# Extra rows of w4 on five DMA engines, wide value matmuls on four column groups, and a reordered tail in a one-token attention kernel

## The chip, the cores and the metric

The kernel runs on one core of a Trainium2 chip. A core has TensorE (PE; its weight loads, which overlap its matmuls, are listed as PEld), VectorE (DVE), ScalarE (ACT), GpSimd (POOL) and SyncE (SP), and 16 DMA engines that move data between memory (HBM) and the on-chip memory. The metric is the device time of one execution in microseconds, the median of several; the profile is of one execution.

## The reference

One token `x` of 512 numbers goes through two branches. Branch A is attention over the last 4096 positions of a cache, with 32 heads of width 128; branch B is a small gated network.

```python
xn = layernorm(x)
# A
q = (xn @ wq)                       # 32 heads x 128
k, v = k_cache[..., -4096:, :], v_cache[..., -4096:, :]
p = softmax(q . k * 128 ** -0.5)
s = concat(p @ v) @ wo              # 4096 -> 512
# B
h = gelu(layernorm(xn) @ w1)        # shifted by one or two tokens: with one token, zeros
x1 = xn + shift(h) @ w2             # so x1 = xn
g = silu(x1 + gelu(layernorm(x1) @ w3) @ w4)   # 512 -> 1376 -> 512
out = x + s * g
```

Everything is bf16 in memory. Keys and values are 32 MB each, wq and wo 4 MB each, w2, w3, w4 and x 3.3 MB: 78.84 MB are read once.

## The kernel before

**Layout.** The heads are taken in 8 groups of G = 4. A group's keys are one tile of 128 partitions by 128 "chunks" of 128 numbers (32 KB in a partition, 4 MB), its values another. `load_kv` (line 97) loads one, whole or in pieces along the chunks (`cuts`); a piece of 64 chunks is 16 KB in each partition. All loads but x's are issued by SP in program order (`load`, line 78), and an issue that must wait for its buffer holds up those behind it. There are three key buffers and two value buffers. The value buffers lie where the first weights (pool `wts`) were, so that the first values wait until queries are made.

**Start.** w2, w3, w4, wq are loaded, then keys. The few operations on x, branch B (lines 177 to 238) and the queries (241 to 258) run meanwhile. w4 is loaded as 10 rows in each of 128 partitions and 96 rows of 1 KB. The planner of the framework orders the operations of this part on each engine; in `manual_schedule` (line 510 on) PE, DVE and ACT run in program order.

**A stage.** Stage `s` (the loop of line 514) takes the keys of group s and the values of group h = s - 2. Of the 128 key chunks DVE takes the first 64 to 80 (`k_vector`, lines 308 and 310: a product and a sum over 128 numbers). For the rest PE turns chunks (line 324), ACT copies them (326) and PE multiplies them with the queries (332). The softmax follows one stage later (`sm_turn`, `sm_exp`, line 370), its denominator (`sm_den`, line 376) two stages later. `v_part` multiplies the probabilities with the values: for most groups as 128 matmuls with the value chunk as stationary operand and four columns moving (line 430), for groups in `MOVED`, here 0 and 2, as 32 matmuls with 16 columns of probabilities stationary and four chunks, 512 columns, moving (line 422); `v_add` (437) then gathers the right four blocks of that result one stage later. `v_out` divides by the denominator.

**Output projection.** The 32 heads are three `blocks`: 16, 8 and 8. For a block `ox_spread` and `ox_pick` (lines 456 to 476) rearrange the heads' outputs so that wo can be loaded with several of its rows in one partition: `y_wide` for block 0 and `y_block` (line 501) for the others, which adds into `y_ps` with four matmuls a row over four column groups (`rows_add`, line 150). Of the last block only 320 rows, `wo_few`, are loaded so: in two loads over an outermost dimension of NE = 5, into 20 partitions each, 8 KB in a partition (line 402), and `ox_few` (line 478) puts the outputs there by a product with the constant `few`. The rest, `wo_rows`, comes as rows of 1 KB, half of head 26 and heads 27 to 31 (`load_rows`); `y_head` multiplies them.

**Tail.** At s = 8 PE runs: softmax of group 7, block 1's `ox_pick` and `y_block(1)`, the sum of block 0's row (line 589), values of group 6, the denominator of group 7, the last block's `ox_pick` and `ox_few`. At s = 9: the first 64 chunks of group 7's values, `y_block` of the few rows, heads 26 and 27, the other chunks, `v_out`, heads 28 to 31. Then the product with `g_row`, the sum with x, the store. SP's order at the end: values 6, rows of heads 26 and 27, values 7 in pieces of 64, 48 and 16 chunks, rows of heads 28 and 29, 30, 31.

Of the kernel before, what the change touches and what calls it, by code (L numbers as in the profile page):

```python
# [8 lines left out]
P = 128  # L9
# [16 lines left out]
MOVED = (0, 2)  # L26
# [3 lines left out]
def kernel(  # L30
# [28 lines left out]
    assert F == 10 * P + 96  # L59
# [30 lines left out]
    w4_sb = wts.tile([P, 11, D], BF16, name="w4_sb")  # L90
    load(w4_sb[:, 0:10, :], B_w4[0:10 * P, :].rearrange("(p c) n -> p c n", p=P))
    load(w4_sb[0:96, 10, :], B_w4[10 * P:F, :])
    wq_sb = wts.tile([P, KC, HD], BF16, name="wq_sb")

    load(wq_sb[:].rearrange("p c n -> p (c n)"), A_wq.rearrange("(a b c) n -> b a (c n)", a=2, c=KC))
# [80 lines left out]

    x_f = small.tile([P, KC], FP32, name="x_f")
# [8 lines left out]
    perm = wts.tile([P, P // 2, 2], BF16, name="perm")  # L186
    nc.vector.tensor_copy(out=perm[:], in_=ident_bf[:].rearrange("k (a b) -> k b a", a=2))
# [24 lines left out]
    chunks = [(P, slice(r, 10 * P, 10)) for r in range(10)]  # L212
    chunks += [(96, slice(10 * P, F, 1))]
    a_ps = ps_misc.tile([P, 11], FP32, tag="misc", name="a_ps")
    for j, (m, cols) in enumerate(chunks):
        for c in range(KC):
            nc.tensor.matmul(a_ps[0:m, j:j + 1], lhsT=w3_sb[:, c, cols], rhs=z3_bf[:, c:c + 1],  # L217
                             start=(c == 0), stop=(c == KC - 1))
    a_bf = small.tile([P, 11], BF16, name="a_bf")
    nc.scalar.activation(out=a_bf[:, 0:10], in_=a_ps[:, 0:10], func=ACT.Gelu_apprx_tanh)  # L220
    nc.scalar.activation(out=a_bf[0:96, 10:11], in_=a_ps[0:96, 10:11], func=ACT.Gelu_apprx_tanh)
# [5 lines left out]
    for i, (m, _) in enumerate(chunks):  # L227
        nc.tensor.matmul(hr_ps[:], lhsT=a_bf[0:m, i:i + 1], rhs=w4_sb[0:m, i, :], start=False,  # L228
                         stop=(i == len(chunks) - 1))
# [31 lines left out]

    few = const.tile([P, 2, 32], BF16, name="few")
    nc.vector.memset(few[:], 0.0)
    for c in range(2):
        nc.vector.tensor_copy(
            out=few[:, c, 0:4 * NE].rearrange("p (a b) -> p a b", b=4),
            in_=ident_bf[:, 4 * NE * c:4 * NE * (c + 1)].rearrange("p (b a) -> p a b", b=4))


# [18 lines left out]
                            op0=ALU.add, op1=ALU.mult)  # L290

# [93 lines left out]
    blocks = [(0, 16), (16, 8), (24, 8)]  # L385
    few_block = 2
    few_h = blocks[few_block][0]
    FEW = 8 * 8 * NE
    h_part = few_h + FEW // P

    r_part = FEW % P
# [6 lines left out]
    def load_few():  # L398
        t = wo_blk[few_block]
        for c in range(2):  # L400
            r0 = few_h * P + c * FEW // 2
            load(t[32 * c:32 * c + 4 * NE],
                 A_wo[r0:r0 + FEW // 2, :].rearrange("(b a t) n -> a b (t n)", b=4, a=NE))

# [3 lines left out]
    def load_rows(h, n):  # L408
        if h == h_part:
            load(wo_rows[r_part:P, 0, :], A_wo[h * P + r_part:(h + 1) * P, :])  # L410
            h, n = h + 1, n - 1
        load(wo_rows[:, h - h_part:h - h_part + n, :],
             A_wo[h * P:(h + n) * P, :].rearrange("(h p) n -> p h n", p=P))
# [3 lines left out]
    def v_part(g, v, c0=0, c1=CP):  # L417
        s = st[g]
        if g in MOVED:
            s["ov"] = ps_o.tile([4 * G, 4, Dh], FP32, tag="oT", name="ov")  # L420
            for c in range(0, CP, 4):
                nc.tensor.matmul(s["ov"][:], lhsT=s["pT"][:, c:c + 4, :].rearrange("p i a -> p (i a)"),  # L422
                                 rhs=v[:, c:c + 4, :], start=(c == 0), stop=(c == CP - 4))
            s["ov_sb"] = sm_pool.tile([4 * G, 4, Dh], FP32, tag="ov_sb", bufs=1, name="ov_sb")
            nc.scalar.copy(out=s["ov_sb"][:], in_=s["ov"][:])  # L425
            return
        if c0 == 0:
            s["oT"] = ps_o.tile([P, G], FP32, tag="oT", name="oT")
        for c in range(c0, c1):
            nc.tensor.matmul(s["oT"][:], lhsT=v[:, c, :], rhs=s["pT"][:, c, :], start=(c == 0),  # L430
                             stop=(c == CP - 1))

    def v_add(g):
        s = st[g]
        s["oT"] = ps_misc.tile([P, G], FP32, tag="misc", name="oT")
        for j in range(4):
            nc.tensor.matmul(s["oT"][:], lhsT=s["ov_sb"][:, j, :], rhs=ident_f[0:4 * G, G * j:G * j + G],  # L437
                             start=(j == 0), stop=(j == 3))

    def v_out(g):  # L440
        h = G * g
        b = [i for i, (h0, _) in enumerate(blocks) if h >= h0][-1]
        if b not in o_blk:
            o_blk[b] = sm_pool.tile([P, blocks[b][1]], BF16, tag=f"o{b}", bufs=1, name="o")
            if b == few_block:
                nc.gpsimd.memset(o_blk[b][:], 0.0)
        c = h - blocks[b][0]
        if g >= NG - 2:
            nc.vector.tensor_tensor(out=o_blk[b][:, c:c + G], in0=st[g]["oT"][:], in1=st[g]["rden"][:],  # L449
                                    op=ALU.mult)  # L450
            return
        for k in range(G):
            nc.scalar.mul(o_blk[b][:, c + k:c + k + 1], st[g]["oT"][:, k:k + 1], st[g]["rden"][:, k:k + 1])  # L453
# [24 lines left out]
    def ox_few(i):  # L478
        of_ps = ps_misc.tile([64, 8], FP32, tag="misc", name="of_ps")
        nc.tensor.matmul(of_ps[:], lhsT=few[:].rearrange("p a b -> p (a b)"), rhs=ox_blk[i][:],  # L480
                         start=True, stop=True)
        of = sm_pool.tile([64, 8], BF16, tag="of", bufs=1, name="of")
        nc.vector.tensor_copy(out=of[:], in_=of_ps[:])
        ox_blk[i] = of


# [14 lines left out]
    def y_block(i):  # L501
        for t in range(8):
            rows_add(y_ps, ox_blk[i][:, t:t + 1], wo_blk[i][:, t, :], False)

    def y_head(h):
        rows_add(y_ps, o_blk[few_block][:, h - few_h:h - few_h + 1], wo_row(h), h == H - 1)

    NG = H // G
    cuts = (0, 64, 112, CP)
# [4 lines left out]
    for s in range(NG + LAG):  # L514
# [3 lines left out]
        if s == LAG:  # L518
            wts_guard.__exit__(None, None, None)
            v_pool = ctx.enter_context(tc.tile_pool(name="v", bufs=V_BUFS))  # L520
            wo_blk[few_block] = v_pool.tile([64, 8, D], BF16, tag="wo_few", bufs=1, name="wo_few")
            nc.gpsimd.memset(wo_blk[few_block][:], 0.0)
            wo_rows = v_pool.tile([P, H - h_part, D], BF16, tag="wo_rows", bufs=1, name="wo_rows")
            nc.gpsimd.memset(wo_rows[0:r_part, 0, :], 0.0)
        if last:
            load_rows(h_part, 2)
# [9 lines left out]
        if h == 5:  # L536
            load_wo(1)
            load_few()
# [41 lines left out]
        elif s == NG:  # L580
# [3 lines left out]
            sm_turn(NG - 1)  # L584
            ox_spread(1)
            sm_exp(NG - 1)
            ox_pick(1)
            y_block(1)
            rows_add(y_ps, one_f, y_row, False)
            v_part(h, v)  # L590
            v_out(h)
            ox_spread(few_block)
            sm_den(NG - 1)
            sm_rden(NG - 1)
            ox_pick(few_block)
            ox_few(few_block)
        else:
            v_part(h, v, 0, cuts[1])
            y_block(few_block)
            for r in range(h_part, H - G):  # L600
                y_head(r)
# [41 lines left out]
```

## Time and profile before

| | us |
|---|---|
| median of 4 runs | 195.05 (194.93 to 196.39) |
| profiled execution | 196.39 |
| its span in the profile | 194.5 |
| PE busy | 133.4 (69%) |
| DVE busy | 143.8 (74%) |
| ACT busy | 87.0 (45%) |
| POOL busy | 6.5 (3%) |
| HBM rate over the span | 405 GB/s |
| values of group 7, first piece issued by SP | 172.73 |
| values of group 6 at PE | 178.80 |
| last matmul of the rows | 191.1 |

The span of the profile is the program on the core; the execution's time holds some 1.9 us more around it. Times on the page and in the timeline are microseconds from the span's start, and "issue" in the chain is time in which an engine waited for nothing that the profile shows. The page gives the busy share in 40 slices of 4.86 us, the chain of work that ended last, and groups of instructions with their mean duration. The timeline lists instructions in order of time with the idle time before them. Where the text speaks of landing marks, they are the marks that each DMA engine sets when its part of a load is in place; a load over all engines has sixteen. Packet durations are of the trace's DMA records, which tell a packet's queue, start, size and duration.

### The profile page before, as it was taken

Reading aid. Unit: us, or ns where it says so; the run is one execution under the profiler, and the core shown is the slowest. Engines: PE = TensorE matmul, PEld = TensorE weight load, DVE = VectorE, ACT = ScalarE, POOL = GpSimd, SP = SyncE. Lnnn points to the kernel's source line nnn. Section 1 sums busy time; section 2 is a strip of 40 time slices with the busy share of each in tenths; the row PEclk is TensorE's granted clock in tenths of the full one; section 3 lists DMA queues with packets and bytes.
Section 4 is the critical chain, followed back from the end, with each engine's and each line's share of the span. In section 5 each row is a group of like instructions: output and inputs, shape, how many; then the busy total and the mean of one; then the engine's idle time right before and its main releaser. Section 6 shows DMA issues by size and latency. Waiting matters only on the chain.

```text
span 194.5 us, 4769 instructions
## 1 busy us (share of the span) xinstructions
PE 133.4 (69%) x2123; PEld 101.9 (52%) x2123; DVE 143.8 (74%) x162; ACT 87.0 (45%) x195; POOL 6.5 (3%) x14
## 2 busy tenths in 40 slices
PE   0559760877856589698898929740788878855782
PEld 0453450766645433487794418730768246744761
DVE  1550119988999999999999999990899989951201
ACT  2003010788896350478678135721475059813000
POOL 2110007000000000000000000000000000000000
PEclk9999855698555558978559985855555599655555
DMA  6999999999999999999999999999999999999980
GB/s 214 415 442 371 377 428 457 431 438 421 438 428 431 438 426 428 431 431 428 425 428 445 421 431 391 472 421 428 425 451 430 425 428 389 470 418 367 425 308 2
DMA packets 4725, 79.13 MB, mean 407 GB/s; under 512 B 666, under 2 KB 1466, under 8 KB 1722
## 3 DMA queue, kind: packets, MB, share of 16 engines
q1 hardware_dynamic: 4554, 78.84, 95.8%
q8 instruction: 16, 0.26, 0.5%
q10 hardware_dynamic: 152, 0.00, 0.0%
q14 instruction: 3, 0.02, 0.0%
HBM read 78.84 MB, written 0.00 MB: 405 GB/s over the span
## 4 chain that ended last, share of the span: by engine, by line
DMA 46%; DVE 34%; PE 11%; ACT 6%; issue 1%; ACTq 0%; SPq 0%
DMA kv<-in_A_k_cache_dram 29%; DVE S L310 20%; DMA kv<-in_A_v_cache_dram 14%; DVE prod L308 11%; PE oT L430 6%; ACT kt L326 5%; PE pt L324 3%; DMA x_bf<-in_A_x_dram 2%; PE y_ps L150 1%; PE sT L332 1%; ACT own L341 1%; DVE S L346 1%; DVE m L348 1%; DVE mx L356 0%; DVE md L358 0%
## 5 line engine op out<-in xcount | busy, mean ns | idle before, releaser
L310 DVE TENSOR_REDUCE S<-prod 128x20 f32<-128x2560 bf16 (+2 forms) x32 | 82.2, 2570 | 1.1
L326 ACT COPY kt<-pt 128x1024 bf16<-128x1024 bf16 (+1 forms) x56 | 54.4, 1007 | 22.6 <-PE pt L324 21.9
L324 PE MATMUL pt<-ident_bf,kv 128*128 128x128 bf16 x444 | 45.1, 268 | 10.3 <-DMA kv<-in_A_k_cache_dram 10.3
L308 DVE TENSOR_TENSOR prod<-kv,q_bc 128x2560 bf16<-128x2560 bf16 (+2 forms) x32 | 43.5, 1359 | 7.9 <-DMA kv<-in_A_k_cache_dram 5.8
L324 PEld LDWEIGHTS <-kv 128*128 128x128 bf16 x444 | 36.5, 123 | 12.4 <-DMA kv<-in_A_k_cache_dram 11.1
L332 PE MATMUL sT<-qT_bf,kt 128*128 128x4 bf16 x444 | 20.6, 168 | 16.6 <-ACT kt L326 15.8
L332 PEld LDWEIGHTS <-kt 128*128 128x128 bf16 x444 | 17.0, 103 | 24.5 <-ACT kt L326 24.4
L430 PE MATMUL oT<-pT,kv 128*128 128x4 bf16 x768 | 22.1, 166 | 6.1 <-issue 4.7
L430 PEld LDWEIGHTS <-kv 128*128 128x128 bf16 x768 | 21.4, 104 | 8.0 <-issue 5.6
L422 PE MATMUL ov<-kv,pT 128*16 128x512 bf16 x64 | 16.5, 423 | 0.0
L370 ACT ACTIVATE pT<-S,mb 128x128 bf16<-128x128 f32 x32 | 13.9, 569 | 0.3
L453 ACT ACTIVATE o<-oT,rden 128x1 bf16<-128x1 f32 x24 | 4.3, 261 | 15.2 <-PE oT L430 8.5
L422 PEld LDWEIGHTS <-pT 128*16 128x16 bf16 x64 | 6.1, 98 | 9.4 <-issue 3.2
L449 DVE TENSOR_TENSOR o<-oT,rden 128x4 bf16<-128x4 f32 x2 | 0.3, 162 | 12.4 <-PE oT L430 12.4
L341 ACT ACTIVATE own<-sT,par 128x48 f32<-128x48 f32 (+2 forms) x32 | 7.6, 361 | 3.7 <-PE sT L332 3.7
L370 ACT ACTIVATION_READ_ACCUMULATOR pT<-S,mb 128x1 f32 x32 | 8.2, 255 | 0.0
L231 DVE COPY hr<-hr_ps 1x512 f32<-1x512 f32 x1 | 0.7, 679 | 8.4 <-PE hr_ps L228 8.4
L496 PE MATMUL yr_ps<-wo,ox 128*1 128x512 bf16 x16 | 6.0, 560 | 0.9 <-DVE ox L474 0.9
L425 ACT COPY ov_sb<-ov 16x512 f32<-16x512 f32 x2 | 1.1, 575 | 12.0 <-PE ov L422 12.0
L437 PE MATMUL oT<-ident_f,ov_sb 16*128 16x4 f32 x16 | 2.9, 301 | 4.3 <-DVE rden L381 4.3
L220 ACT ACTIVATE a_bf<-a_ps 128x10 bf16<-128x10 f32 x1 | 0.2, 180 | 11.8 <-PE a_ps L217 11.8
L363 PE MATMUL mb_ps<-md,par_t 5*128 5x4 f32 x16 | 4.0, 316 | 1.7 <-DVE md L358 1.0
(117 smaller groups left out, 92.6 us busy)
## 6 DMA issues: line engine op xcount, KB each, us to landing
kv<-in_A_k_cache_dram SPq DMA_DIRECT2D x7, 4096.0 KB, 30.5
kv<-in_A_v_cache_dram SPq DMA_DIRECT2D x7, 4096.0 KB, 34.8
wq_sb<-in_A_wq_dram SPq DMA_DIRECT2D x1, 4096.0 KB, 19.7
kv<-in_A_k_cache_dram SPq DMA_DIRECT2D x2, 2048.0 KB, 25.2
wo<-in_A_wo_dram SPq DMA_DIRECT2D x1, 2048.0 KB
kv<-in_A_v_cache_dram SPq DMA_DIRECT2D x1, 2048.0 KB, 11.4
kv<-in_A_v_cache_dram SPq DMA_DIRECT2D x1, 1536.0 KB, 14.4
w_sb<-in_B_w_dram SPq DMA_DIRECT2D x1, 1376.0 KB
```

The lines of the kernel that those rows point to most:

```text
L308: nc.vector.tensor_tensor(out=prod[:, 0:m, :], in0=kn[:, rows, :], in1=q_bc[:, g:g + 1, :].to_broadcast([P, m, Dh]), op=ALU.mult)
L310: nc.vector.tensor_reduce(out=st[g]["S"][:, rows], in_=prod[:, 0:m, :], axis=AX.X, op=ALU.add)
L324: nc.tensor.transpose(pt[:, c - c0, :], kn[:, c, :], ident_bf[:])
L326: nc.scalar.copy(out=kts[b][:, 0:c1 - c0, :], in_=pt[:, 0:c1 - c0, :])
L332: nc.tensor.matmul(st[g]["sT"][:, c - nd(g), :], lhsT=kt[:, c - c0, :], rhs=qT_bf[:, G * g:G * g + G], start=True, stop=True)
L341: nc.scalar.mul(s["own"][:, 0:m, a], s["sT"][:, 0:m, a], par[:, a:a + 1])
L363: nc.tensor.matmul(mb_ps[:], lhsT=par_t[:].rearrange("k b a -> k (b a)"), rhs=md[:], start=True, stop=True)
L370: nc.scalar.activation(out=s["pT"][:, :, a], in_=s["S"][:], func=ACT.Exp, scale=scale, bias=mb[:, a:a + 1], accum_out=s["sum"][:, a:a + 1])
L422: nc.tensor.matmul(s["ov"][:], lhsT=s["pT"][:, c:c + 4, :].rearrange("p i a -> p (i a)"), rhs=v[:, c:c + 4, :], start=(c == 0), stop=(c == ...
L430: nc.tensor.matmul(s["oT"][:], lhsT=v[:, c, :], rhs=s["pT"][:, c, :], start=(c == 0), stop=(c == CP - 1))
L453: nc.scalar.mul(o_blk[b][:, c + k:c + k + 1], st[g]["oT"][:, k:k + 1], st[g]["rden"][:, k:k + 1])
L496: nc.tensor.matmul(yr[i][:], lhsT=ox_blk[i][:, t:t + 1], rhs=wo_blk[i][:, t, :], start=(t == 0), stop=(t == n - 1))
```

## The change

w4 is loaded as 8 rows in each of 128 partitions, 32 rows of 1 KB, and 320 extra rows in the manner of `wo_few`: `w4_few`, cleared by POOL, in two loads over five. w3's columns are taken in the matching order, so the hidden numbers are 17 columns and not 11, and the product with `few` (which moves up) puts the last eight in their places. wq's rows are laid in four parts and not two. wo's last eight heads become a block of 4 (`wo_4`, 128 partitions) and 4 heads of 1 KB rows. Groups 0 to 5 are all `MOVED`; their 32 wide matmuls now write four column groups in turn, 32 partitions apart, after a matmul of zeros that clears the tile, and `v_add` sums the four with the constant `fold`. In the tail, `v_out` of groups 5 on is DVE's, the values of group 6 come ahead of `y_block(1)`, `ox_pick(2)` stands behind the first 64 chunks of group 7, and group 7's values come in pieces of 64, 32, 16 and 16 chunks.

```diff
-MOVED = (0, 2)
+MOVED = (0, 1, 2, 3, 4, 5)
...
-    w4_sb = wts.tile([P, 11, D], BF16, name="w4_sb")
-    load(w4_sb[:, 0:10, :], B_w4[0:10 * P, :].rearrange("(p c) n -> p c n", p=P))
-    load(w4_sb[0:96, 10, :], B_w4[10 * P:F, :])
+    w4_sb = wts.tile([P, 9, D], BF16, name="w4_sb")
+    load(w4_sb[:, 0:8, :], B_w4[0:8 * P, :].rearrange("(p c) n -> p c n", p=P))
+    load(w4_sb[0:32, 8, :], B_w4[F - 32:F, :])
+    w4_few = wts.tile([64, 8, D], BF16, name="w4_few")
+    nc.gpsimd.memset(w4_few[:], 0.0)
+    for c in range(2):
+        f0 = 8 * P + 32 * NE * c
+        load(w4_few[32 * c:32 * c + 4 * NE],
+             B_w4[f0:f0 + 32 * NE, :].rearrange("(b a t) n -> a b (t n)", b=4, a=NE))
...
-    load(wq_sb[:].rearrange("p c n -> p (c n)"), A_wq.rearrange("(a b c) n -> b a (c n)", a=2, c=KC))
+    load(wq_sb[:].rearrange("p c n -> p (c n)"), A_wq.rearrange("(a b c) n -> b a (c n)", a=4, c=KC))
...
+    chunks = [P] * 8 + [32] + [8 * NE] * 8
+    a_ps = ps_misc.tile([P, 17], FP32, tag="misc", name="a_ps")
+    for j, m in enumerate(chunks):
         for c in range(KC):
-            nc.tensor.matmul(a_ps[0:m, j:j + 1], lhsT=w3_sb[:, c, cols], rhs=z3_bf[:, c:c + 1],
+            nc.tensor.matmul(a_ps[0:m, j:j + 1], lhsT=w3_cols(c, j), rhs=z3_bf[:, c:c + 1],
                              start=(c == 0), stop=(c == KC - 1))
...
+    nc.scalar.activation(out=a_bf[0:8 * NE, 9:17], in_=a_ps[0:8 * NE, 9:17], func=ACT.Gelu_apprx_tanh)
+    af_ps = ps_misc.tile([64, 8], FP32, tag="misc", name="af_ps")
+    nc.tensor.matmul(af_ps[:], lhsT=few[0:8 * NE].rearrange("p a b -> p (a b)"), rhs=a_bf[0:8 * NE, 9:17],
+                     start=True, stop=True)
+    af_bf = small.tile([64, 8], BF16, name="af_bf")
+    nc.vector.tensor_copy(out=af_bf[:], in_=af_ps[:])
...
+    fold = const.tile([P, 32], FP32, name="fold")
+    nc.vector.tensor_reduce(out=fold[:], in_=ident_f[:].rearrange("p (q m) -> p m q", m=32), axis=AX.X,
+                            op=ALU.max)
...
-    blocks = [(0, 16), (16, 8), (24, 8)]
+    blocks = [(0, 16), (16, 8), (24, 4), (H - G, G)]
+    h_part = H - G
...
-            s["ov"] = ps_o.tile([4 * G, 4, Dh], FP32, tag="oT", name="ov")
-            for c in range(0, CP, 4):
-                nc.tensor.matmul(s["ov"][:], lhsT=s["pT"][:, c:c + 4, :].rearrange("p i a -> p (i a)"),
-                                 rhs=v[:, c:c + 4, :], start=(c == 0), stop=(c == CP - 4))
+            s["ov"] = ps_o.tile([P, 4, Dh], FP32, tag="oT", name="ov")
+            nc.tensor.matmul(s["ov"][:], lhsT=zero_bf[:], rhs=zero_bf[:].unsqueeze(1).to_broadcast([P, 4, Dh]),
+                             start=True, stop=False, skip_group_check=True)
+            for i in range(CP // 4):
+                c, r = 4 * i, 32 * (i % 4)
+                nc.tensor.matmul(s["ov"][r:r + 4 * G], lhsT=s["pT"][:, c:c + 4, :].rearrange("p i a -> p (i a)"),
+                                 rhs=v[:, c:c + 4, :], start=False, stop=(i >= CP // 4 - 4),
+                                 skip_group_check=True)
...
-            nc.tensor.matmul(s["oT"][:], lhsT=s["ov_sb"][:, j, :], rhs=ident_f[0:4 * G, G * j:G * j + G],
+            nc.tensor.matmul(s["oT"][:], lhsT=s["ov_sb"][:, j, :], rhs=fold[:, G * j:G * j + G],
...
-        if g >= NG - 2:
+        if g >= NG - 3:
...
-    cuts = (0, 64, 112, CP)
+    cuts = (0, 64, 96, 112, CP)
...
-            wo_blk[few_block] = v_pool.tile([64, 8, D], BF16, tag="wo_few", bufs=1, name="wo_few")
-            nc.gpsimd.memset(wo_blk[few_block][:], 0.0)
+            wo_blk[2] = v_pool.tile([P, 4, D], BF16, tag="wo_4", bufs=1, name="wo_4")
...
-            load_rows(h_part, 2)
             v = load_kv(v_pool, A_v_cache, h, cuts)
...
             load_wo(1)
-            load_few()
+            load_wo(2)
...
             sm_turn(NG - 1)
+            sm_exp(NG - 1)
+            v_add(h - 1)
+            v_out(h - 1)
             ox_spread(1)
-            sm_exp(NG - 1)
             ox_pick(1)
+            v_part(h, v)
+            v_out(h)
+            ox_spread(2)
             y_block(1)
             rows_add(y_ps, one_f, y_row, False)
-            v_part(h, v)
-            v_out(h)
-            ox_spread(few_block)
             sm_den(NG - 1)
             sm_rden(NG - 1)
-            ox_pick(few_block)
-            ox_few(few_block)
         else:
             v_part(h, v, 0, cuts[1])
-            y_block(few_block)
-            for r in range(h_part, H - G):
-                y_head(r)
+            ox_pick(2)
+            y_block(2)
             for c0, c1 in zip(cuts[1:], cuts[2:]):
                 v_part(h, v, c0, c1)
             v_out(h)
```

## The prediction

> **What bounds the kernel.** I read the page's slices first, then the queues, then the chain at its end, then the timeline around it.
>
> ```profile
> span 194.5 us, 4769 instructions
> ...
> DMA  6999999999999999999999999999999999999980
> GB/s 214 415 442 371 377 428 457 431 438 421 438 428 431 438 426 428 431 431 428 425 428 445 421 431 391 472 421 428 425 451 430 425 428 389 470 418 367 425 308 2
> ...
> q8 instruction: 16, 0.26, 0.5%
> ```
>
> The loads run from end to end. Every one is issued before its predecessors have landed; the closest is the last values' first piece, issued at 172.73, when the earliest of the 16 engines runs out at 175.2 (its part of the rows before). So a faster compute stage in the middle buys nothing. What can move the end is the work per DMA engine and the chain behind the last values. That chain, in order of time:
>
> ```profile
> 150.71 28.04 DMA kv<-in_A_v_cache_dram
> 178.75 0.05 issue
> 178.80 2.21 PE oT L430 x77
> 181.01 0.13 issue
> 181.14 1.52 PE oT L430 x51
> ...
> 184.34 1.80 PE oT L430 x64
> 186.14 0.41 PE y_ps L150 x9
> 186.55 0.78 issue
> 187.32 1.11 PE y_ps L150 x27
> 188.44 1.81 PE oT L430 x64
> ...
> 190.49 0.62 PE y_ps L150 x15
> ```
>
> TensorE is busy nearly throughout from 178.8 (values of group 6, "V6") to 191.11. The loads' landing marks end in a tie with it: V7's pieces land at 184.12, 187.76 and 188.99, the rows of heads 28-31 at 189.62, 189.94 and 190.26. The result leaves 3.4 us after the last row of the chain.
>
> The "issue" pieces are the other thing to see. q8 brings TensorE's instructions, 16 KB or 256 instructions at a time. I numbered TensorE's instructions in order of time: its unexplained stops before numbers 1729, 2497, 3521, 3777 and 4033 are all multiples of 256 apart, each ending 1.3 to 1.5 us after a q8 packet of 1.05 us. The stop of 187.32 is packet 184.95, the stop of 181.14 packet 178.62. A packet starts 3.4 to 6.2 us after TensorE comes near the block before (1.7 for the very last one, among small loads). A block is 128 matmuls with their weight loads, 3.6 us when dense, so dense stretches outrun the fetch.
>
> ```profile
> 172.43 0.18 PEld L430 LDWEIGHTS <-kv 128*128 128x128 bf16 x4 [1.38 <-issue]
> ...
> 176.06 1.02 PE L150 MATMUL y_ps<-wo,ox 128*1 128x128 bf16 x32 [0.62 <-DVE ox L474]
> ```
>
> **The loads.** Packet durations in the trace: 1 KB 46 ns, 4 KB 159, 8 KB 309, 10 KB 385, 16 KB 613, 32 KB 1213. Each `wo_few` load leaves five landing marks, where others leave sixteen: five engines carry it. Per engine:
> - w4: before 8x385 + 6x46 = 3.36 us on all. After 8x309 + 2x46 = 2.56 on eleven engines and 2.47 more (8x309, the few rows) = 5.03 on five.
> - wo's end: before 12x46 ahead of V7 and 32x46 behind it, plus 2.47 of `wo_few` on five. After 8x159 = 1.27 ahead of V6, 32x46 behind.
>
> The total is 0.08 us less on every engine, and the unevenness moves from 167 us to 10 us. Until V6 the eleven engines are 0.79 early and the five 1.67 late; V6 lands 0.47 later (+1.27-0.79 or +1.67-2.47+1.27): 179.2. V7's first piece 184.05, its quarter of 32 chunks 2.47 later, then 1.27 each, the last row 190.2. Fewer TensorE instructions (below) mean 14 fetches, not 16. They do not move the end: the late engines are the five, some of which also took another instruction packet.
>
> The Trainium skill, "DMA: Bandwidth & Descriptors", section on rules for kernel authors, warns that an outermost dimension below 16 confines a load to that many engines, which speaks against the new w4 load. By it 1.7 us (2.47 against 0.79 spread out) is lost on five engines. As the same five lose the same in `wo` before, it cancels in my sum.
>
> **The start.** The `w4_few` load waits for a POOL memset of 64x4096; the same shape is in the trace:
>
> ```profile
> 28.79 3.50 POOL L522 MEMSET wo_few<- 64x4096 bf16 x1 [16.57 <-PE qb_ps L256]
> ```
>
> From 0.9 it ends at 4.4 (behind the identities 5.3). SP stands meanwhile, with wq and the first keys behind it. w2, w3 and w4 keep the engines fed until about 10.2, so it costs nothing; if the memset stood behind the layernorm's power (7.97 us), SP would be free at 11.5 and the eleven engines idle for some 4 us. TensorE gets 24 more small matmuls (24 x 63 ns = 1.5), 6 of 512 wide (1.3 to 2.6), the `few` product with its copy (0.5): queries and DVE's first product at 31.6, not 28.95. wq's landing at 23.95 is under that. DVE idles 5.8 us for K6 at 131, which takes it up. `perm` and wq's order change no packet size: 0. A third set of masks, `fold` and the moved `few` are some 0.3 us each on a waiting DVE: 0.
>
> **Groups 1, 3, 4, 5.** 128 narrow matmuls become one of zeros, 32 of 512 wide and 4 fp32 ones in the sum of column groups. No row shows 512 wide over column groups. Bounds: one at a time they run 427 ns apart at the granted clock of 0.50 and 215 at 1.0 (L422's starts), so 33x0.427 = 14.1 us at worst; fully side by side 33x0.215/4 = 1.8. I choose by L150, which does use four column groups: 32 of 128 wide in 1.02 us, 32 ns each where one by itself would take 427/4 = 107. A factor 3.3: 33x0.427/3.3 = 4.3 us. V5 starts at 167.67 and frees its buffer at 172.0, before it did at 172.7 (with its fetch stop): V7's issue stays ahead. The early groups stay covered by 10 us and more of queued loads; the fp32 sums (1.05 us for 8 at 82.18) lie beside transposes there.
>
> The skill's "TensorE: Matmul & The Clock Gate", Part 3, measured 2.38x for three column groups. By that V5 would end at 173.6, still ahead of 175.2.
>
> **The tail, step by step** (starts, from the rows above). V6 179.25, 3.5 without a stop (before 3.70): 182.75. `y_block(1)` and the y_row sum, which stood in idle time at 176 and now stand behind V6: 0.95+0.6: 184.3. `den` of two fp32 0.55: 184.85. Now V7's first 64, landed long ago, 1.80 by themselves. Instruction numbers: 340 matmuls less (380 in groups 1, 3, 4, 5, 16+8 of the few block and its rows, 1 of `ox_few` gone; 24+6+1+2+32 come), 680 instructions; V6 starts at number 2912, as 40 matmuls moved behind it. Blocks begin at 193+256k: 3009 is inside V6 and comes in time, 3265 is six matmuls into V7. Its fetch is asked for near 180.25 (25 instructions ahead) and takes 3.6+2.4: 186.25, where TensorE is there at 185.0. A stop of 1.25. V7a ends 187.9; `ox_pick(2)` stands between matmuls, with the DVE round trip 0.83+0.1: 188.8 (it was there before, with `ox_few` behind it); 16 matmuls 0.48: 189.3; the other 64 of V7 1.88: 191.2, all landed by 189.1 and the next block (3521) asked for at 186.25, here about 190.4; o 0.24; 16 for the rows 0.62: 192.05.
>
> Before, that was 191.11: +0.9 us, of which landing +0.45, V6 -0.2, moved block against idle time +0.3, the new stop +1.25, few block, its rows and their stop -0.9. The profiled execution took 196.39 (span 194.5 and 1.9 around it) against a median of 195.05; the step is added to the median: **195.9 us**, 0.4% slower. A measurement of this kernel tells about 1% from no change.
>
> **Rivals.**
> - *The fetch comes in time; the loads bound the end.* Then the rows of head 31 at 190.2, 0.3 for its matmuls: 190.5 against 191.11, less by 0.65: 194.4. For it: fewer instructions, and the small pieces are asked for later in the run; against it: every dense 256 from 167 us on stopped in the trace. 0.20.
> - *The fetch takes as long as the one of 178.62* (entered 172.43, running again 181.14: 8.7, not 6.0). The stop grows by 2.6: 198.5; halfway 197.2. It decides from 8 us on. 0.12.
> - *Column groups run one after another* (slower): V5 lasts 14.1, to 181.8; SP holds V7 back, the engines run dry from 175.2 on, first packets near 183.7, then 11.3 of pieces and rows: 195.0+0.3 against 191.11, +4.2: 199.3. It decides when V5 takes over 8 us. For it L422's 427 ns apart, against it L150. 0.06.
> - *SP's wait at the start shows* (memset late): +4, 199. 0.04.
> - *The tail's reordering does nothing and landings shift by chance*: 195.0. Inside the forecast.
>
> **Chances.** Forecast (194.7 to 196.9) 0.58, the first rival 0.20, slower ones 0.22. The range leaves out the two dearest: 194.3 to 198.0. Faster by over 1% (under 193.1) needs the last landing itself over 1 us earlier, 0.04; slower by over 1% (over 197.0) 0.18; the rest 0.78.
>
> **What would show it.** Fourteen q8 packets; V6 landing near 179.2; a TensorE line "issue" of about 1 us inside V7's first 64; the last rows at 192, 1.8 us behind the last landing; 33 matmuls in about 4 us for group 5 and SP's issue of V7 near 172. Wrong would be: no stop there, a V6 landing below 178.5, or an SP issue after 175.

## The result and the profile after

The changed kernel takes **195.89 us** (median of 53 runs, 195.53 to 197.29), the kernel before 195.09 (79 runs beside them, 194.31 to 197.46): a ratio of 1.0036, with a 95% interval of 1.0026 to 1.0047. It is 0.8 us slower.

The queues and slices of the page, changed kernel:

```profile
span 193.9 us, 4090 instructions
...
DMA  6999999999999999999999999999999999999960
GB/s 213 412 430 433 426 433 433 428 433 429 433 429 434 433 429 433 433 433 433 429 433 429 433 433 399 463 433 433 429 433 428 429 433 385 470 426 389 404 248 4
...
q8 instruction: 14, 0.23, 0.5%
```

The loads still run from end to end, with fourteen packets of instructions. TensorE's timeline around the last values (start, duration, what; in brackets the idle time ahead and what ended it):

```profile
168.66 1.90 PE L431 MATMUL ov<-kv,pT 128*16 128x512 bf16 x32
...
178.21 3.57 PE L440 MATMUL oT<-pT,kv 128*128 128x4 bf16 x128 [3.04 <-DMA kv<-in_A_v_cache_dram]
181.71 1.02 PE L156 MATMUL y_ps<-wo,ox 128*1 128x128 bf16 x32
...
183.64 0.30 PE L440 MATMUL oT<-pT,kv 128*128 128x4 bf16 x6
184.65 1.68 PE L440 MATMUL oT<-pT,kv 128*128 128x4 bf16 x58 [0.71 <-issue]
...
187.38 1.57 PE L440 MATMUL oT<-pT,kv 128*128 128x4 bf16 x53
189.20 0.43 PE L440 MATMUL oT<-pT,kv 128*128 128x4 bf16 x11 [0.25 <-issue]
189.89 0.59 PE L156 MATMUL y_ps<-wo_rows,o 128*1 128x128 bf16 x16 [0.26 <-DVE o L457]
```

V6 starts as it lands. There are two stops with "issue" behind them. The first is six matmuls into V7, ahead of instruction 3265, as the prediction had it; the second, eleven matmuls before V7's end, is ahead of 3521, where it had none. The packets that end them start at 182.27 and 186.73, last 1.10, and TensorE runs again 1.3 and 1.4 us after they have ended.

The first profile of before (execution 196.39, 1.3 above the median) cannot be set against this one (execution 195.80, near its median): by it the change would have gained. The kernel before was therefore profiled again (the experiment *b_again*), in an execution of 195.00. The end of its chain:

```profile
149.36 28.20 DMA kv<-in_A_v_cache_dram
...
177.61 3.68 PE oT L430 x128
...
182.97 1.83 PE oT L430 x64
184.79 0.41 PE y_ps L150 x9
185.20 0.75 issue
185.95 1.12 PE y_ps L150 x31
187.06 1.81 PE oT L430 x64
...
189.12 0.63 PE y_ps L150 x10
```

and the end of the changed kernel's:

```profile
178.21 3.57 PE oT L440 x128
181.78 1.48 PE y_ps L156 x40
183.27 0.52 PE den_ps L397 x2
183.78 0.16 PE oT L440 x6
183.94 0.71 issue
184.65 1.68 PE oT L440 x58
...
187.45 1.50 PE oT L440 x53
188.95 0.25 issue
189.20 0.45 PE oT L440 x11
...
189.89 0.63 PE y_ps L156 x13
```

Start minus start gives each step of the tail:

| step (us) | before, again | after | difference | predicted |
|---|---|---|---|---|
| V6 starts | 177.61 | 178.21 | +0.60 | +0.45 |
| V6's matmuls | 3.68 | 3.57 | -0.11 | -0.2 |
| V6's end to V7's first 64 | 1.68 | 2.00 | +0.32 | +0.3 |
| V7's first 64, with a stop | 1.82 | 2.56 | +0.74 | +1.25 |
| from there to V7's other 64 | 2.27 | 1.11 | -1.16 | -0.9 |
| the other 64, with a stop | 1.82 | 2.20 | +0.38 | 0 |
| `v_out`, to the last rows | 0.24 | 0.24 | 0 | 0 |
| last rows start | 189.12 | 189.89 | **+0.77** | **+0.9** |

The result row is issued at 190.41 and 191.19, +0.78; the medians differ by 0.80.

### The profile page after: what moved, and what is told of

Read it like the earlier page. It is cut to its first block, busy times and chain, and to the rows that moved or that the text cites. A ratio compares the mean times of both kernels' runs of the same rounds, so it can differ in the third digit from the quotient of the medians.

```text
span 193.9 us, 4090 instructions
## 1 busy us (share of the span) xinstructions
PE 136.0 (70%) x1783; PEld 100.2 (52%) x1783; DVE 145.2 (75%) x168; ACT 90.0 (46%) x196; POOL 5.9 (3%) x12
## 4 chain that ended last, share of the span: by engine, by line
DVE 41%; DMA 26%; PE 25%; issue 4%; ACT 2%; POOL 0%; POOLq 0%; ACTq 0%; SPq 0%
DVE S L331 23%; DMA kv<-in_A_v_cache_dram 13%; DVE prod L329 13%; DMA kv<-in_A_k_cache_dram 11%; PE oT L440 4%; PE pt L345 3%; PE hr_ps L255 3%; PE oT L447 3%; PE a_ps L236 2%; DMA x_bf<-in_A_x_dram 2%; PE qT_ps L271 2%; PE ov L431 2%; PE y_ps L156 1%; ACT kt L347 1%; PE sT L353 1%
## 5 line engine op out<-in xcount | busy, mean ns | idle before, releaser
L347 ACT COPY kt<-pt 128x1024 bf16<-128x1024 bf16 (+1 forms) x56 | 55.2, 1005 | 16.3 <-PE pt L345 15.2
L345 PE MATMUL pt<-ident_bf,kv 128*128 128x128 bf16 x444 | 50.6, 290 | 2.9 <-DMA kv<-in_A_k_cache_dram 2.9
L345 PEld LDWEIGHTS <-kv 128*128 128x128 bf16 x444 | 41.3, 134 | 7.4 <-DMA kv<-in_A_k_cache_dram 3.8
L431 PE MATMUL ov<-kv,pT 128*16 128x512 bf16 x192 | 19.5, 578 | 0.0
L447 PE MATMUL oT<-fold,ov_sb 128*128 128x4 f32 x48 | 9.8, 328 | 13.0 <-DVE rden L402 12.8
L447 PEld LDWEIGHTS oT<-fold,ov_sb 128*128 128x128 f32 x48 | 9.3, 288 | 13.5 <-DVE rden L402 13.2
L461 ACT ACTIVATE o<-oT,rden 128x1 bf16<-128x1 f32 x20 | 3.6, 264 | 20.3 <-PE oT L447 20.3
L440 PE MATMUL oT<-pT,kv 128*128 128x4 bf16 x256 | 7.6, 166 | 4.0 <-DMA kv<-in_A_v_cache_dram 3.0
L440 PEld LDWEIGHTS <-kv 128*128 128x128 bf16 x256 | 7.4, 105 | 5.1 <-DMA kv<-in_A_v_cache_dram 3.8
L435 ACT COPY ov_sb<-ov 128x512 f32<-128x512 f32 x6 | 3.5, 589 | 9.1 <-PE ov L431 9.1
L375 PE MATMUL mt_ps<-ident_f,m 128*1 128x128 f32 x8 | 2.9, 360 | 4.4 <-DVE rden L402 4.4
```

Source lines behind the costliest of these rows:

```text
L345: nc.tensor.transpose(pt[:, c - c0, :], kn[:, c, :], ident_bf[:])
L347: nc.scalar.copy(out=kts[b][:, 0:c1 - c0, :], in_=pt[:, 0:c1 - c0, :])
L431: nc.tensor.matmul(s["ov"][r:r + 4 * G], lhsT=s["pT"][:, c:c + 4, :].rearrange("p i a -> p (i a)"), rhs=v[:, c:c + 4, :], start=False, sto ...
L447: nc.tensor.matmul(s["oT"][:], lhsT=s["ov_sb"][:, j, :], rhs=fold[:, G * j:G * j + G], start=(j == 0), stop=(j == 3))
```

## The experiments

All change a few lines of one of the two kernels. "Before" with a run is the kernel before on the same chip in the same hour; it moved between 195.18 and 195.38 from one such set to another.

**b_again: the kernel before, unchanged.** Its first profile has V6 landing at 178.75. Is that the kernel, or that execution?

> The kernel before, unchanged, profiled once more. Its first profile is of an execution of 196.39 us, 1.3 above its median, and the 32 KB packets of wq took 1.1 us more per engine there than elsewhere. Theory (the first profile was of a dear execution, and its excess lies in wq's load): if this execution is near 195.1, wq's load shows an excess near 0, the values of group 6 land near 177.5 instead of 178.75 and the span is about 193.2. Rival (the excess is in the tail): wq's excess is again about 1.1 us and the tail's stops are shorter.

Measured: 195.04 (194.64 to 195.91). V6 landed at 177.56, 1.19 earlier than in the first profile. Each packet's duration less the usual one of its size, summed per engine, is 1.3 us more in the first profile, and that much is in wq's 32 KB packets, which start between 10.5 and 20.4 us: 112 of the 128 take about 1400 ns there, against the usual 1213. The absolute times of the prediction's first profile were those of a dear execution; the differences between kernels were not touched by that.

**b_wq4 and a_wq2: the order of wq's rows alone**, four parts in the kernel before, two in the changed one.

```diff
-    load(wq_sb[:].rearrange("p c n -> p (c n)"), A_wq.rearrange("(a b c) n -> b a (c n)", a=2, c=KC))
+    load(wq_sb[:].rearrange("p c n -> p (c n)"), A_wq.rearrange("(a b c) n -> b a (c n)", a=4, c=KC))
...
-    perm = wts.tile([P, P // 2, 2], BF16, name="perm")
-    nc.vector.tensor_copy(out=perm[:], in_=ident_bf[:].rearrange("k (a b) -> k b a", a=2))
+    perm = wts.tile([P, P // 4, 4], BF16, name="perm")
+    nc.vector.tensor_copy(out=perm[:], in_=ident_bf[:].rearrange("k (a b) -> k b a", a=4))
```

> The kernel before with wq's rows laid in four parts and not two (and the matching perm). Theory (the two-part order makes some executions dear, by up to 1.3 us): the median goes down by 0.1 to 0.4 us, and executions above 196 us go away. Rival (the order of wq's rows costs nothing, as I predicted): 195.1, the same spread as before.

> The changed kernel with wq's rows laid in two parts, as before. Theory (as above): median up by 0.1 to 0.4 us, to 196.0 to 196.3, and some executions 1 us and more above. Rival: 195.9 with the narrow spread of the changed kernel.

Measured: 195.36 beside 195.38 before, ratio 1.0009 (0.998 to 1.0038); and 195.88, ratio 1.0037 (1.002 to 1.0053), which is the changed kernel's own. The order of wq is worth nothing either way; executions above 196 remain with four parts (196.56, 196.87). The one dear execution of *a_wq2* is the profiled one (197.69), and there wq's packets take the usual time (1217 ns in the mean), so its excess is not in wq. In *b_shift98*, with two parts, they take 1342 ns in the mean, in *b_again*, with two parts too, 1213: what makes them long in some executions stays open.

**a_shift48: 48 matmuls of zeros ahead of V6.** Their result is not used. They move every instruction behind them by 96 numbers, and so the place at which a new block begins.

```diff
             ox_pick(1)
+            idle = ps_tr.tile([P, G], FP32, tag="pt", name="idle")
+            for _ in range(48):
+                nc.tensor.matmul(idle[:], lhsT=zero_bf[:], rhs=ident_bf[:, 0:G], start=True, stop=True)
             v_part(h, v)
```

> The changed kernel with 48 matmuls of zeros (96 instructions, nothing reads their result) ahead of group 6's values, where TensorE waits for the load. They move the begin of every later 256-instruction block: from 97, 353 and 609 instructions behind the first matmul of group 6 to 1, 257 and 513. Theory (the stops at 183.94 and 188.95 are waits for instruction blocks): both stops go, 0.71 and 0.25 us; the rows of heads 28 to 31 are then bound by the last landing near 189.4; 195.0 to 195.2. Rival (the stops have another cause, or the values' landing bounds the tail): 195.9, with the stops at the same matmuls as in the changed kernel.

Measured: **197.14** (194.89 to 198.32), ratio 1.0066 (1.0035 to 1.0098): wrong in sign. TensorE's timeline:

```profile
177.86 1.44 PE L588 MATMUL idle<-ident_bf,zero_bf 128*128 128x4 bf16 x48
179.16 3.55 PE L440 MATMUL oT<-pT,kv 128*128 128x4 bf16 x128
184.53 1.02 PE L156 MATMUL y_ps<-wo,ox 128*1 128x128 bf16 x32 [1.82 <-issue]
...
191.47 0.59 PE L156 MATMUL y_ps<-wo_rows,o 128*1 128x128 bf16 x16 [0.25 <-DVE o L457]
```

The stop moved with the block: it stands at number 3265 again, which is now just behind V6, and it is the only one left. But it is dearer, 1.82, and in this execution the matmuls of zeros were not hidden, as block 1's pick came only at 177.83 (174.96 in the changed kernel's profile): V6 had landed at 178.08 and started at 179.16. The last rows start 1.58 later than in the changed kernel's profile; 0.95 of that is V6's later start, and 0.63 the stretch from there to the last rows (12.31 against 11.68). Every instruction has a number 96 higher, and yet the packet starts at 181.92, hardly earlier than the 182.27 of the changed kernel. The block before it, 3009, begins one instruction behind the one that waits for V6. A request that is not made before that wait has ended would explain the late packet, and the times agree with it: the packet starts 2.76 us after V6's start, the changed kernel's 2.7 us after TensorE comes to 3009, 97 instructions into V6. It was not tried apart from the rest. That a stop belongs to a block held; the price of this place and of the matmuls themselves was not foreseen. The run's spread is wide, and the profile shows its dear side: the four executions under 196.1 have a mean granted clock of 0.70 to 0.71, the six from 197.23 on one of 0.65 to 0.69.

**a_shift69 and a_shift69b: 69 matmuls of zeros in stage 3**, far from the tail. The blocks then begin 41 instructions ahead of V6, and 215 and 471 behind its start.

```diff
             k_open(s)
             k_vector(s, kn, 0)
+            if s == 3:
+                idle = ps_tr.tile([P, G], FP32, tag="pt", name="idle")
+                for _ in range(69):
+                    nc.tensor.matmul(idle[:], lhsT=zero_bf[:], rhs=ident_bf[:, 0:G], start=True, stop=True)
```

> The changed kernel with 69 matmuls of zeros (138 instructions, about 2 us, nothing reads them) at the begin of stage 3, where TensorE has idle time. The instruction blocks of the tail begin 41 instructions ahead of group 6's first matmul (inside group 5's values, so the next block is asked for some 8 us before group 6's landing) and 215 and 471 behind it. Theory (the tail is bound by the arrival of instruction blocks, and a block is asked for when TensorE's sequencer comes to the one before, which it cannot while it stands at a wait): no stop at 215, at most 0.4 us at 471 (asked for near 181, there 5.4 us later, used at 186.1); the last landing at 189.4 bounds the rows; 195.0 to 195.3. Rival (bound by landings and work alone): 195.9.

> The changed kernel with 69 unused matmuls of zeros in stage 3 once more, beside another 5 rounds of the kernel before. Theory (where the instruction blocks begin makes the change's loss): 195.1 to 195.4, ratio within 0.9985 to 1.0015. Rival (the first comparison was chance, the loss is in the landings and the tail's work): 195.8, ratio 1.003 to 1.004.

Measured: 195.22 beside 195.31 before, ratio 1.0000 (0.9973 to 1.0027), and the second time 195.02 beside 195.25, ratio 1.001 (0.999 to 1.0031). Added work that is of no use takes the change's loss away in the median. But the 24 executions do not lie together: sixteen are between 194.88 and 195.34, all below the lowest of the changed kernel's 53 (195.53), and eight between 195.74 and 197.34. The mean granted clock does not separate them: 0.651 to 0.725 in the sixteen, 0.650 to 0.699 in the eight. Both profiles are of the dearer group (195.74 and 195.82). The first:

```profile
169.36 3.59 PE L431 MATMUL ov<-kv,pT 128*16 128x512 bf16 x32
...
178.25 3.58 PE L440 MATMUL oT<-pT,kv 128*128 128x4 bf16 x128
...
183.68 1.85 PE L440 MATMUL oT<-pT,kv 128*128 128x4 bf16 x64
185.39 0.17 PE L476 MATMUL ox_ps<-spread,to 128*128 128x16 bf16 x1
187.26 0.60 PE L156 MATMUL y_ps<-wo,ox 128*1 128x128 bf16 x16 [1.70 <-DMA wo_rows<-in_A_wo_dram]
```

V7's first 64 run through, as wanted. The 1.70 ahead of 187.26 is named after a load that landed last by the profile, but the group's first matmul is number 3521, where a block begins; its packet starts at 184.70. Behind `ox_pick` the changed kernel waits 0.48 for DVE, so about 1.2 of the 1.70 is a stop. Even with one stop in the place of two, this execution starts its last rows at 189.91, as the changed kernel does. What the cheaper sixteen executions do is not in a profile.

**b_shift98: the same for the kernel before**, 98 matmuls of zeros (`zero_bf`, results unused) ahead of the first stage; blocks again begin 215 and 471 instructions behind V6's first.

```diff
+    idle = ps_tr.tile([P, G], FP32, tag="pt", name="idle")
+    for _ in range(98):
+        nc.tensor.matmul(idle[:], lhsT=zero_bf[:], rhs=ident_bf[:, 0:G], start=True, stop=True)
     for s in range(NG + LAG):
```

> The kernel before with 98 matmuls of zeros (196 instructions, 2.8 us) ahead of the first stage, where TensorE waits 4.8 us for keys. The tail's blocks begin 41 ahead of group 6's first matmul and 215 and 471 behind it, not 155 and 411 behind it. Theory: the stop of 0.8 to 1.05 us inside the few rows' block goes or shrinks under 0.4; the last landing at 189.0 then bounds the rows; 194.5 to 194.8. Rival (the stop is not a wait for instructions, or landings bound the end already): 195.1.

Measured: 194.86 (194.5 to 196.16) beside 195.31, ratio 0.999 (0.9966 to 1.0014). By the times it cannot be told from the kernel before. TensorE's timeline, of a dear execution (195.84) with V6 landing at 178.71:

```profile
178.75 3.58 PE L430 MATMUL oT<-pT,kv 128*128 128x4 bf16 x128 [2.53 <-DMA kv<-in_A_v_cache_dram]
...
185.91 1.02 PE L150 MATMUL y_ps<-wo_few,of 64*1 64x128 bf16 x32
...
187.55 0.27 PE L150 MATMUL y_ps<-wo_rows,o 128*1 128x128 bf16 x1 [0.32 <-issue]
...
189.87 0.66 PE L150 MATMUL y_ps<-wo_rows,o 128*1 128x128 bf16 x16 [0.26 <-DVE o L449]
```

The stop of 0.75 inside the few rows has gone; one of 0.32 stands where the next block begins, as expected. From V6's start to the last rows it is 11.12 us, in *b_again* 11.51. In the trace, then, the kernel before also pays for its blocks, some 0.4 us; in the total that is not shown.

**a_early: `y_block(1)` and the y_row sum ahead of V6**, as in the kernel before.

```diff
+            y_block(1)
+            rows_add(y_ps, one_f, y_row, False)
             v_part(h, v)
             v_out(h)
             ox_spread(2)
-            y_block(1)
-            rows_add(y_ps, one_f, y_row, False)
```

> The changed kernel with block 1's matmuls and the sum of block 0's row ahead of group 6's values again, as in the kernel before. Theory (tail chain): 1.55 us of TensorE's work leave the chain behind group 6's landing; but the instruction blocks then begin 17, 273 and 529 instructions behind group 6's first matmul, and as TensorE's sequencer stands at that matmul until the load lands, the block at 273 is asked for at the landing only, 6 us ahead of its use at 182.5: a stop of 1.2 to 1.7 us. Together 0.2 to 0.5 less than the changed kernel: 195.4 to 195.7. Rival (only the landings bound the tail): 195.9, no change. Rival (no waits for instructions): 195.0.

Measured: 196.05 (195.73 to 197.11), ratio 1.0048 (1.002 to 1.0075). No gain. TensorE's timeline:

```profile
178.96 1.02 PE L156 MATMUL y_ps<-wo,ox 128*1 128x128 bf16 x32 [0.62 <-DVE ox L482]
...
180.44 3.57 PE L440 MATMUL oT<-pT,kv 128*128 128x4 bf16 x128
...
185.54 1.69 PE L440 MATMUL oT<-pT,kv 128*128 128x4 bf16 x58 [0.94 <-issue]
```

V6 had landed at 178.32 and waited behind a block 1 whose outputs were not there: with group 5 wide, its gathering (1.87 us at 175.75) comes first. In the kernel before the same product ran at 174.68, in idle time. In this execution, where group 5's values take 3.59, that cover has gone. In the changed kernel's profile they take 1.90 and block 1's pick comes at 174.96; whether the cover is there in such an execution of *a_early* is not in a profile. The time cannot be told from the changed kernel's; the order of the kernel before is no better here.

**a_wo4late: the load of `wo_4` behind V6** instead of ahead of it, so that V6 lands earlier.

```diff
         if h == 5:
             load_wo(1)
+        if h == NG - 2:
             load_wo(2)
```

> The changed kernel with the load of wo's block of 4 heads behind group 6's values instead of ahead of them. Group 6's values land 1.27 us earlier, at 176.9, all later loads as in the changed kernel. Theory (the rebalanced loads cost through group 6's later landing, as TensorE's chain starts there): the chain starts 1.2 us earlier and the last landing at 189.4 becomes the bound; 195.0 to 195.3. Rival (the tail does not depend on group 6's landing): 195.9.

Measured: 195.86 (195.64 to 196.12), ratio 1.0033 (1.0015 to 1.005). V6 landed at 176.98 and started at 177.22, 1.0 earlier than in the changed kernel, and nothing came of it. TensorE's timeline:

```profile
177.22 3.58 PE L440 MATMUL oT<-pT,kv 128*128 128x4 bf16 x128
...
183.89 1.69 PE L440 MATMUL oT<-pT,kv 128*128 128x4 bf16 x58 [0.37 <-issue]
...
189.27 0.43 PE L440 MATMUL oT<-pT,kv 128*128 128x4 bf16 x11 [0.80 <-issue]
189.96 0.59 PE L156 MATMUL y_ps<-wo_rows,o 128*1 128x128 bf16 x16 [0.26 <-DVE o L457]
```

V7's first 64 resume 0.76 earlier than in the changed kernel, but the second stop takes it back, 0.80 where it was 0.25: the packet that ends it starts at 186.79, in the changed kernel at 186.73. In this execution this block's arrival, not V6's landing, sets the end.

**a_narrow: only groups 0 and 2 wide**, the same groups as in the kernel before, but on column groups; group 5's gathering at the tail goes, the rest of the change stays.

```diff
-MOVED = (0, 1, 2, 3, 4, 5)
+MOVED = (0, 2)
...
-            v_add(h - 1)
-            v_out(h - 1)
             ox_spread(1)
```

> The changed kernel with groups 0 and 2 alone as wide matmuls on column groups; 1, 3, 4, 5 as 128 narrow ones, as before. Theory (no stage in the middle bounds anything; the wide groups change only where the instruction blocks begin): group 6's first matmul is number 3608, blocks begin 169 and 425 behind it; the stop moves to 84 matmuls... of instructions into group 7's first 64 chunks, 0.6 to 0.9 us, and there is none later: 195.6 to 195.9; 16 instruction packets of q8. Rival (wide groups on column groups save time): 196.5 and more. Rival (they cost time, by their fp32 sums): under 195.4.

Measured: 195.78 (195.44 to 195.96), ratio 1.003 (1.0013 to 1.0047). The wide groups save matmuls and no time. There are sixteen instruction packets again and one stop in the tail:

```profile
186.09 0.73 PE L440 MATMUL oT<-pT,kv 128*128 128x4 bf16 x22 [0.97 <-issue]
...
189.99 0.59 PE L156 MATMUL y_ps<-wo_rows,o 128*1 128x128 bf16 x16 [0.26 <-DVE o L457]
```

**a_serial: the wide matmuls all on one column group**, the prediction's dear rival made real.

```diff
-                c, r = 4 * i, 32 * (i % 4)
+                c, r = 4 * i, 0
```

> The changed kernel with all 32 wide matmuls of a group on the first column group, so that they cannot run side by side; the work is the same. Theory (my rival in the prediction: without overlap the value stage of group 5 holds back the last values' load): group 5's values take 7 us (granted clock 1.0) to 14 us (0.5) instead of 1.9 to 3.6; the last values are issued at 176 to 182 instead of 170.6 to 173, the DMA engines run dry; 196.4 at the short end, 199.3 at the long one. Rival (loads are queued far enough ahead): 195.9.

Measured: **208.96** (208.01 to 209.71), ratio 1.0701 (1.0656 to 1.0746). The rate of the page's slices and TensorE's timeline:

```profile
GB/s 222 447 419 420 433 442 419 436 452 417 401 463 430 420 417 455 436 408 436 449 424 408 430 452 430 405 442 446 424 419 422 431 433 344 6 0 303 375 239 3
```

```profile
176.43 9.81 PE L431 MATMUL ov<-kv,pT 128*16 128x512 bf16 x32
```

V5 takes 9.8 us, V7's load is issued at 186.28 and not at 170.61, and the engines are empty for two slices. The mechanism is the rival's; its price is three times the rival's +4.2, because V5 does not start at 168 but at 176.4: the five wide groups ahead of it take 8.05 to 9.71 us each, in the changed kernel 3.32 to 3.59, and the stages behind them come late as well.

**a_best: narrow groups, `wo_4` behind V6, and 105 unused matmuls of zeros in stage 3**, that is the group edit and the load edit above together, and the blocks at 215 and 471 behind V6's first instruction.

```diff
-MOVED = (0, 1, 2, 3, 4, 5)
+MOVED = (0, 2)
...
+        if h == NG - 2:
             load_wo(2)
...
+            if s == 3:
+                idle = ps_tr.tile([P, G], FP32, tag="pt", name="idle")
+                for _ in range(105):
+                    nc.tensor.matmul(idle[:], lhsT=zero_bf[:], rhs=ident_bf[:, 0:G], start=True, stop=True)
...
-            v_add(h - 1)
-            v_out(h - 1)
             ox_spread(1)
```

> The changed kernel with groups 1, 3, 4 and 5 narrow again (only 0 and 2 wide), the load of wo_4 behind the values of group 6 instead of ahead, and 105 matmuls of zeros in stage 3, whose results are not used, so that TensorE's instruction blocks begin 215 and 471 instructions behind the first of the values of group 6 (numbers 4033 and 4289). Theory (instruction blocks end the change's tail, and what is left of the loss is the late start of the values of group 6): values of group 6 landed and started near 177.1, stops of 0.6 or less, the last row's matmuls then bound by the last landing mark (189.4), out issued near 190.2 against 190.41 of a typical execution before: 194.6 to 194.9, beside 195.1 to 195.3 before. Rival (the landings or the work of the tail's new pieces bound it, the blocks do not): like the narrow kernel, 195.6 to 195.9.

Measured: **194.99**, all twelve executions between 194.87 and 195.07, beside 195.25 before; ratio 0.9983 (0.9962 to 1.0004). TensorE's timeline:

```profile
176.96 3.58 PE L440 MATMUL oT<-pT,kv 128*128 128x4 bf16 x128 [4.04 <-DMA kv<-in_A_v_cache_dram]
...
183.09 1.87 PE L440 MATMUL oT<-pT,kv 128*128 128x4 bf16 x64 [0.55 <-DMA kv<-in_A_v_cache_dram]
...
186.00 1.44 PE L440 MATMUL oT<-pT,kv 128*128 128x4 bf16 x48
188.09 0.59 PE L440 MATMUL oT<-pT,kv 128*128 128x4 bf16 x16 [0.65 <-DMA kv<-in_A_v_cache_dram]
188.93 0.73 PE L156 MATMUL y_ps<-wo_rows,o 128*1 128x128 bf16 x16 [0.25 <-DVE o L457]
```

No stop is left behind V6. TensorE waits for landings, first for V7's first piece and then for its last 16 chunks, and the result row is issued at 190.35, 0.84 before the changed kernel's. This is 0.9 us under the changed kernel's median, and 0.1 above the expected 194.6 to 194.9, since the last landing that counts is not the last row (189.34) but V7's last piece (188.04), with 16 chunks, `v_out` and the rows behind it. It beats the changed kernel; from the kernel before it cannot be told apart.

## Why the prediction was right

The time, 195.9, and its reason hold: the end is set by TensorE's chain behind the last values, and a fresh instruction block stands in it. That the figure was hit to 0.01 is luck, as two of its terms were off by 0.4 to 0.5 in opposite directions. Point by point:

- **The loads.** V6's landing +0.47 predicted, +0.61 measured (177.56 to 178.17). Fourteen packets, as counted. The last row was to land 0.06 earlier (190.2 for 190.26) and lands 0.36 later (189.38 for *b_again*'s 189.02); why is open. It bounds nothing here, as the last rows start at 189.89.
- **The numbering.** The stop before 3265, six matmuls into V7, is where it was predicted. It is the finest test of the numbering of instructions, and it came from counting the diff's matmuls alone.
- **The size of that stop** was 0.71 for 1.25. TensorE stood there 5.73 after V6's start (5.75 predicted), and ran 2.4 after the packet's start, as estimated. The mis-sized term is the 3.6 from request to packet: counted as the prediction counts it, 1.0 behind V6's start, the request is at 179.2 and the packet at 182.27, 3.1. The term is a spread and no constant: other profiles have stops of 0.37 (*a_wo4late*), 0.94 (*a_early*) and 1.10 (*a_wq2*, the execution of 197.69) ahead of the same instruction.
- **"The next block (3521) asked for at 186.25, here about 190.4"**, no stop: this step failed. Only the 1.7 of "the very last one" gives 190.4; with the 3.6 of the first stop it would have been 192.25, and a stop. Its packet started at 186.73, 2.1 after TensorE entered the block before it, and the block was there at 189.20, 4.55 after that; TensorE had come to it at 188.95, 4.3 after. Small here, but *a_wo4late* shows that this arrival bounds the end. The sum came out right by luck: this miss (0.38 too little in the last 64) and that of the first stop (0.5 too much) nearly cancel.
- **Adding the terms.** The sum treats landing, moved block and stops as independent. They are not: in *a_wo4late* a gain of 0.99 at V6's start is 0.44 at V7's (which waits 0.41 for its landing), 0.76 behind the first stop, and -0.07 behind the second. The wait for V7's landing took a part of the gain, the first stop was shorter (0.37 for 0.71) and gave some back, and the second was longer (0.80 for 0.25) and took the rest.
- **The absolute base.** Its times were those of a dear execution, 1.2 late at V6. Taking the step from the profile and adding it to the median kept that out of the forecast.
- **Groups 1, 3, 4, 5.** V5 4.3 predicted, 1.90 measured at a granted clock of 1.0 and 3.59 at 0.50; V7 issued at 170.61. The bound of full overlap was the right one. The Trainium skill, "TensorE: Matmul & The Clock Gate", Part 3, gives 2.38x for three column groups; here four start per 427 ns or per 215 ns, the time that one takes alone at the same clock. *a_narrow* confirms the zero for the time.
- **The start.** The memset ends at 4.38 (4.4 predicted) and costs nothing; DVE's first product is at 33.06, not 31.6. The prediction's own terms, added to 28.95, make 32.25 at least; w3's matmuls are 68 and take 4.78, before 44 in 2.76: +2.0 where +1.5 was put. The loads run from end to end even so, and V7 is issued at 170.61, so it is hidden. wq's order: 0, shown twice.
- **The rivals.** "The fetch comes in time; the loads bound the end": not so in the changed kernel, but *a_best* shows the state that it describes, at 195.0 and not 194.4. The step that was off there is the last landing that counts: V7's last 16 chunks and what stands behind them, not head 31's row. Column groups one after another: mechanism shown, 199.3 for 208.96.

What the loss consists of: the changed kernel with narrow groups, `wo_4` later and no stop behind V6 (*a_best*) takes 194.99, the change 195.89. The first two of these edits have no effect alone (195.78, 195.86); the two together without the shift were not run, so how the gain divides between the block places and these edits is not shown. The shift alone (*a_shift69*, both times) brings the median to 195.0 to 195.2, and that is the evidence for the block places by themselves. Why eight of its executions stay at 195.7 or more is open. Their two profiles show a slow V5 and a stop of 1.2 at number 3521; the slow V5 (3.59) stands in *a_wo4late*'s profile too, at that run's median (195.86). Whether the cheaper executions lack either is not in a profile.

A page bears on this. The Trainium skill, "Runtime: NRT & Kernel Launch", section on instruction fetch mechanics, states that the sequencer fetches the next 16 KiB block of 256 instructions over a DMA queue of its own while it runs the current one, and that the crossing is "mostly hidden". The block size is what the numbering shows. The hiding holds for some crossings: the one at 3009, inside V6, costs nothing (128 matmuls in 3.57). It does not hold for others: with the engines' queues full of loads, those that show a stop in the tails above cost 0.25 to 1.82 us.

## What to carry to other kernels

Where loads fill the DMA engines and one engine runs dense small instructions, number its instructions, find one such stop and mark every 256th from there: those are places where it can stop for about a microsecond. Shift them, with idle instructions far ahead or by the order of the work, so that the dense stretch behind the last landings runs through, and only then judge an edit of the tail. Profile a second execution of the old kernel before comparing two traces: here the first one differed from a usual one by more than the change is worth.

## What the runs showed that was not expected

- A boundary one instruction behind V6's wait made the dearest stop, 1.82 us (*a_shift48*). Of the 1.25 us by which that run is over the changed kernel (197.14 against 195.89), a part is the 1.44 us of matmuls themselves, which V6's wait did not cover in the execution profiled.
- The same 32 wide matmuls take 1.90 us in one profile and 3.59 in others, four starting per 215 or 427 ns; the granted clock is 1.00 in the one stretch and 0.50 in the other (*a_shift69*). V7 is issued 2.4 later then (172.99 against 170.61), and block 1's pick comes at 177.96 and not at 174.96, just ahead of V6; by these two executions (195.74 and 195.80) it does not show in the total.
- wq's 32 KB packets took about 1400 ns, not 1213, in the first profile of before, and V6 landed 1.2 us later than in *b_again*; in *b_shift98*'s profile they were long as well, and V6 landed at 178.71.
- Twelve executions of *a_best* lie within 0.2 us, of *a_shift69* within 2.4. That a tail bound by landings repeats better is not shown: *a_wo4late*, with two stops behind V6, lies within 0.5 and *a_narrow*, with one, within 0.52.
